# A causal convolution and a two-layer feed-forward block: accumulators copied out in the order they lie, and part of the activation moved from VectorE to ScalarE

## The chip, the cores and the metric

The kernel runs on one core of a Trainium2 chip. Its time is what the device takes for one execution, in microseconds (us); the kernel before has a median of 2262.58 us over three runs (2262.18 to 2262.81). A core has TensorE (PE; PEld is its weight load), VectorE (DVE), ScalarE (ACT), GpSimd (POOL) and SyncE (SP, which here issues nearly all transfers). Each engine works through its own list of instructions in order, and waits where an instruction needs another engine's result.

## The reference

Input x has 8 sequences of 4096 tokens with 192 channels in fp32. Each of 8 groups of 24 channels has a causal convolution of 7 taps whose weights are a softmax. A feed-forward layer follows on all 32768 tokens:

```python
h = x @ w_in                       # 192 -> 2048
beta = 1.0
neg = h <= -beta
pos = h >= beta
g = np.where(pos, h, np.where(neg, 0.0, (h + beta) ** 2 / (4.0 * beta)))
return (g @ w_out).astype(np.float32)   # 2048 -> 192
```

The function g equals max(h, (clip(h, -1, 1)/2 + 1/2)^2). It also equals max(h, min(relu(h/2 + 1/2)^2, 1)).

## The kernel before

The tokens are cut into 64 superblocks of 512, and the 2048 hidden channels into 8 pairs of tiles of 128. One step, numbered q, treats one pair for one superblock; there are 512 steps, and two superblocks (sixteen steps) make a block, because the convolution's work is planned over two superblocks. "Step k" below means q modulo 16.

In step q TensorE runs `mm1(q)` (L422), which puts h for two tiles (128 x 1024) in PSUM, and then `mm2(q - 2)` (L462), which adds the second layer's products to four accumulator banks, accm twice and accr twice. The fp32 values are split in a high and a low fp32r part, so mm1 has eighteen matmuls and mm2 twenty, on half the rows of the array each, two at a time. There are two buffers for h, three each for g, gh and gl.

The activation of a step is made by five instructions over 128 x 1024 values: `act_clip` on VectorE (L473, reads h from PSUM), `act_square` on ScalarE (L479, square of g/2 + 1/2), `act_max` on VectorE (L484, reads h again and gives its buffer back), `act_hi` on ScalarE (L491, the cast to the high part gh) and `act_lo` on VectorE (L497, the low part gl). The last two belong to q - 1. In the main loop the order on ScalarE is thus cast(q - 1), square(q), and on VectorE clip(q), low part(q - 1), max(q).

Around these the loop places the convolution for later tokens (`conv_slot`, by tables of step numbers: products on ScalarE at L219 and L226, sums on GpSimd at L230, transposes on VectorE at L147, the split into parts at L248 and L262, whose halves SP swaps with transfers).

When a superblock's eight steps are done, `evac` copies its four accumulator banks to SBUF (L513, ScalarE) behind the square of step 1 or 9, so that the mm2 of step 2 or 10 can start the next sums. From the third superblock on, TensorE works on the tokens in another order than they lie in memory (`turns`, `both`), and L513 restores an order: it reads a bank in sequence and writes each value to a place that is far from the one before. GpSimd adds the two halves (L515), `evac_rest` moves 64 channels (L525), and `store` turns 32 x 32 tiles around on VectorE (L538) and writes 32 channels at a time with one transfer (L542).

In the first eight steps the kernel makes the activation in another way, which has its own helpers: relu(h/2 + 1/2) and square on ScalarE (L757, L759), and `most` on VectorE (L764), which takes min(g, 1) and the max with h in one instruction.

Of the kernel before, what the change touches and what calls it, by code (L numbers as in the profile page):

```python
# [13 lines left out]
AF = mybir.ActivationFunctionType  # L14
# [6 lines left out]
SQ = 32  # L21
# [9 lines left out]
def lightconv_then_ffn(ctx: ExitStack, tc: tile.TileContext, x, weight, w_in, w_out, out):  # L31
# [24 lines left out]
    nc = tc.nc  # L56
# [8 lines left out]
    NPAIR = NF // 2  # L65
# [44 lines left out]
    def load_unit(c, u, engs=None):  # L110
        ta, tb = 2 * c * TB, (2 * c + 1) * TB
        if u == "rb":
            return load_raw([tb, tb, tb + TB // 2, tb + TB // 2], [P, P + SQ, P, P + SQ], engs,
                            TB // 2)
        if u == "r":
            return load_raw([ta, ta, tb, tb], [P, P + SQ, P, P + SQ], engs)
        return load_raw([ta if u == "a" else tb] * 4, [0, SQ, 2 * SQ, 3 * SQ], engs)
# [5 lines left out]
    def let_go():  # L123

        if pending:
            out, a, b = pending.pop(0)
            nc.vector.memset(warm, 0.0)
            nc.gpsimd.memset(warm, 0.0)
            nc.gpsimd.tensor_add(out, a, b)


    NF32 = 2 * NPAIR
# [257 lines left out]
    NQ = NSB * NPAIR  # L390
    hs, g32, gs, ghs, gls, accs = {}, {}, {}, {}, {}, {}
# [8 lines left out]
    def in_turns(s):  # L400
        return s * NPAIR >= NF32

    def mm1(q):

        s, j = divmod(q, NPAIR)

        if q == 0:
            h = hs[q] = [ps_o.tile([P, TB], F32, name=n) for n in ("accr1", "accm0")]
        else:
            h = hs[q] = ps_h.tile([P, 2, TB], F32, name="h")  # L410
            h = [h[:, e, :] for e in range(2)]

        if s == 0:
            mms = [(WI[j], us, [xop[s][u] for u in us]) for us in ("ns", "sn", "rr")]
        else:
            mms = [(W[j][:, part], u + u, [xop[s][u, x]] * 2) for u in "nsr"
                   for part, x in ((0, "hi"), (1, "hi"), (0, "lo"))]
        for n, (w, us, x) in enumerate(mms):
            for e in range(2):
                c0 = COL[us[e]][e]  # L420
                to, of = (both(h[e]), turns(x[e][e])) if in_turns(s) else (h[e], x[e][e])
                nc.tensor.matmul(to, w[HALVES[e], c0:c0 + P], of,  # L422
                                 start=(n == 0), stop=(n == len(mms) - 1))
# [5 lines left out]
    def mm2_first(q):  # L429


        s, j = divmod(q, NPAIR)
        g, w = g32.pop(q), WF[j + LAG]
        if j == 0:
            new_accs(s)
        for e in range(2):
            for b in range(TB // P):
                a, c0 = "mr"[b // 2], b % 2 * D
                for i, half in enumerate(HALVES):
                    nc.tensor.matmul(accs[s][a, i][:, c0:c0 + D], g[half, e, b * P:(b + 1) * P],  # L440
                                     w[half, e, :], start=(j == 0 and e == 0 and b % 2 == 0),
                                     stop=(j == NPAIR - 1 and e == 1 and b % 2 == 1))
# [24 lines left out]
    def tiles(q):  # L467
        return [slice(0, 1), slice(1, 2)] if q == NQ - 1 else [slice(0, 2)]

    def act_clip(q):  # L470
        g = gs[q] = act.tile([P, 2, TB], F32, name="g", bufs=3)
        for e in tiles(q):
            nc.vector.tensor_scalar(out=g[:, e, :], in0=hs[q][:, e, :], scalar1=-1.0, scalar2=1.0,  # L473
                                    op0=ALU.max, op1=ALU.min)

    def act_square(q):
        g = gs[q]
        for e in tiles(q):
            nc.scalar.activation(g[:, e, :], g[:, e, :], AF.Square, bias=0.5, scale=0.5)  # L479

    def act_max(q):
        h, g = hs.pop(q), gs[q]
        for e in tiles(q):
            nc.vector.tensor_tensor(out=g[:, e, :], in0=h[:, e, :], in1=g[:, e, :], op=ALU.max)  # L484
        if q < NF32:
            g32[q] = gs.pop(q)

    def act_hi(q):
        gh = ghs[q] = act.tile([P, 2, TB], F32R, name="gh", bufs=3)
        for e in tiles(q):  # L490
            nc.scalar.copy(gh[:, e, :], gs[q][:, e, :])  # L491
# [9 lines left out]
    def evac(s):  # L501

        acc = accs.pop(s)
        n = slice(0, 2 * D if s * NPAIR < NF32 else TB)
        for a in "mr":
            t = [ob.tile([P, TB], F32, name="t", bufs=4) for _ in range(2)]
            y = ob.tile([P, TB], F32, name="sum")
            for i in range(2):
                to, of = t[i][:, n], acc[a, i][:, n]
                if in_turns(s):  # L510
                    to = to.rearrange("p (b o a) -> p a b o", b=2, o=2)
                    of = of.rearrange("p (a b o) -> p a b o", b=2, o=2)
                nc.scalar.copy(to, of)  # L513
            if s > 0:
                nc.gpsimd.tensor_add(y[:, n], t[0][:, n], t[1][:, n])  # L515
            else:
                late.append((y[:, n], t[0][:, n], t[1][:, n]))
            sums[s, a] = y
# [9 lines left out]
    def store(s, a, *engs):  # L528
        engs = engs or (nc.sync,)
        y = sums.pop((s, a))  # L530
        if s * NPAIR < NF32:
            t0 = s * TB + (0 if a == "m" else 2 * P)
            engs[0].dma_start(out=out[t0:t0 + 2 * P].rearrange("(b p) d -> p b d", p=P),
                              in_=y[:, 0:2 * D].rearrange("p (b d) -> p b d", b=2))
            return
        n = P if a == "m" else DR
        osb = ob.tile([P, TB // SQ, SQ], F32, name="osb")
        nc.vector.transpose(out=osb[0:n].rearrange("p j b -> p (j b)"), in_=y[0:n])  # L538
        for i in range(n // SQ):
            c0 = i * SQ + (0 if a == "m" else P)  # L540
            dst = out[s * TB:(s + 1) * TB, c0:c0 + SQ]
            engs[i % len(engs)].dma_start(out=dst.rearrange("(j a) b -> a j b", a=SQ),  # L542
                                          in_=osb[i * SQ:(i + 1) * SQ])

    def diagonal(t, *bases):
        nc.gpsimd.memset(t, 0.0)
# [195 lines left out]
    def parts_hi(q):  # L742
        for n, rest in PARTS.get(q, ()):
            chunks[n].hi(rest)
# [17 lines left out]
    def most(h, g):  # L762

        nc.vector.scalar_tensor_tensor(out=g, in0=g, scalar=1.0, in1=h, op0=ALU.min, op1=ALU.max)  # L764
# [75 lines left out]
    for q in range(NQ + DELAY):  # L840
        s, j = divmod(q, NPAIR)
        c, i = divmod(q, 2 * NPAIR)
        done = q - DELAY
        if q < NQ and i == 0 and c > 0:
            conv_b = conv_n["b"]
        if q < NQ and i == (0 if c > 0 else 4):
            conv_n = {}
            if c + 1 < NB:
                conv_n = {u: Conv(c + 1, u, load_unit(c + 1, u)) for u in "arb"}


        if q == NPAIR:
            mm2_first(done)
        if q < NQ:
            mm1(q)
        if done >= 0 and q != NPAIR:
            (mm2 if done >= NF32 else mm2_first)(done)

        if q < 2:
            (step_0, step_1)[q]()  # L860
        elif q < NPAIR:
            first_step(q)
        else:
            if q - 1 in gs:
                act_hi(q - 1)
            if q == NPAIR + 1:
                evac(0)
            if q == 2 * NPAIR - 2:
                pending.extend(late)
            if q < NQ:  # L870
                let_go()
                act_clip(q)
                act_square(q)
            if done % NPAIR == NPAIR - 1 and done >= NPAIR:
                (evac if done < NQ - 1 else evac_last)(done // NPAIR)
            parts_hi(q + 1)
            if q - 1 in gs:
                act_lo(q - 1, nc.vector)
            parts_lo(q, (True,))
            if q < NQ:  # L880
                let_go()
                act_max(q)
                parts_lo(q, (False,))
                conv_slot(i, conv_b, conv_n.get("a"), conv_n.get("r"))

            m, r = (DELAY, DELAY + 1) if s > 1 else (NPAIR - 2, NPAIR - 1)
            if q < NQ and j == m:
                evac_rest(s - 1)
                store(s - 1, "m")
            elif q < NQ and j == r:  # L890
                store(s - 1, "r")
        if q < NQ and i == 2 * NPAIR - 1 and conv_n:
            conv_n["b"].transpose()
        if q == NQ - 4:
            plain = ob.tile([P, TB // SQ, SQ], F32, name="osb").rearrange("p j b -> p (j b)")[:, 0:P]
            diagonal(plain, 0)
# [26 lines left out]
```

## Time and profile before

| What | Value |
|---|---|
| median of three runs | 2262.58 us (2262.18 to 2262.81) |
| the profiled execution | 2263.56 us, of which the span of its instructions is 2261.8 us |
| granted TensorE clock | 1.00 |
| busy: PE, DVE, ACT, POOL | 97%, 92%, 79%, 51% of the span |
| L513, 512 columns | 244 copies, 1079 ns (accm) and 1113 ns (accr) each |
| clip L473, max L484, low part L497 | 503, 503, 495 instructions; 1200, 1217, 1467 ns |
| square L479, cast L491 | 503, 495 instructions; 1058, 1046 ns |
| stores of 64 KB | 366, landing 1.9 us after issue (median) |

A row of the groups gives line, engine, operation, the names written and read, and after the bar the busy us, the mean ns of one, and how long the engine had stood idle before it and for whom. A row of the timeline begins with the start and the length in us, with idle time in square brackets. A row of the stretches gives the busy time of each engine with the number of its instructions.

### The profile page before, as it was taken

The numbers are of one execution on the slowest core, as the hardware profiler recorded it, in microseconds if no ns is written. First come the engines' busy times: TensorE is split into PE (matmuls) and PEld (weight loads), VectorE is DVE, ScalarE is ACT, GpSimd is POOL, SyncE is SP. The second block draws the span as 40 slices with busy tenths as digits, with TensorE's granted clock in tenths as the row PEclk, the third lists the DMA queues.
The fourth block names the chain that finished last, engine by engine and source line by source line (L and its number), as shares of the span: only waits on it lengthen the run. The fifth ranks groups of instructions, "written<-read, shape, count | busy, mean of one in ns | idle before, by whom it ended". The sixth has DMA issues, their size and how long they took to land.

```text
span 2261.8 us, 48144 instructions
## 1 busy us (share of the span) xinstructions
PE 2189.4 (97%) x19646; PEld 1862.2 (82%) x19646; DVE 2077.1 (92%) x1883; ACT 1785.3 (79%) x2153; POOL 1148.6 (51%) x868
## 2 busy tenths in 40 slices
PE   9999999999999999999999999999999999999999
PEld 6988888888888888888888888888888888888887
DVE  8899999999999999999999999999999999999998
ACT  7787877778877788777887787877878778788775
POOL 1455644556545565444654455644556445565451
PEclk9999999999999999999999999999999999999999
DMA  6222122221222212222122222222221222212211
GB/s 158 49 51 51 38 53 44 47 53 38 51 48 46 53 34 51 49 49 51 41 44 48 49 50 48 42 48 44 51 53 39 51 49 45 54 34 51 49 32 27
DMA packets 442125, 110.84 MB, mean 49 GB/s; under 512 B 410288, under 2 KB 417840, under 8 KB 441904
## 3 DMA queue, kind: packets, MB, share of 16 engines
q1 hardware_dynamic: 441744, 107.66, 24.2%
q8 instruction: 155, 2.54, 0.5%
q14 instruction: 66, 0.54, 0.1%
q10 hardware_dynamic: 160, 0.10, 0.0%
HBM read 32.84 MB, written 25.17 MB: 26 GB/s over the span
## 4 chain that ended last, share of the span: by engine, by line
DVE 26%; ACT 23%; PE 20%; issue 14%; POOL 12%; SPq 3%; DMA 1%; POOLq 0%; DVEq 0%; ACTq 0%
POOL y L230 11%; PE h L422 9%; DVE g L484 8%; ACT t L513 8%; DVE g L473 8%; DVE gl L497 7%; ACT g L479 6%; ACT gh L491 5%; PE accm L462 5%; PE accr L462 4%; DVE osb L538 2%; SPq L95 2%; ACT p L219 2%; POOL lo L252 2%; DMA raw<-in_x_dram 1%
## 5 line engine op out<-in xcount | busy, mean ns | idle before, releaser
L230 POOL TENSOR_TENSOR y<-y,p 128x512 f32<-128x512 f32 x546 | 799.8, 1465 | 757.9 <-DVE g L484 539.8
L497 DVE TENSOR_TENSOR gl<-g,gh 128x1024 fp32r<-128x1024 f32 (+1 forms) x497 | 727.5, 1464 | 151.4 <-ACT gh L491 140.4
L491 ACT CAST gh<-g 128x1024 fp32r<-128x1024 f32 (+1 forms) x497 | 519.2, 1045 | 253.9 <-DVE g L484 248.7
L422 PE MATMUL h<-hi,w 64*128 64x512 f32 x4032 | 701.6, 377 | 0.0
L479 ACT ACTIVATE g<-g 128x1024 f32<-128x1024 f32 (+1 forms) x505 | 533.6, 1057 | 161.3 <-DVE g L473 151.0
L462 PE MATMUL accm<-gh,w 64*128 64x512 f32 x3968 | 614.0, 381 | 48.0 <-ACT t L513 48.0
L484 DVE TENSOR_TENSOR g<-h,g 128x1024 f32<-128x1024 f32 (+1 forms) x505 | 613.4, 1215 | 8.2 <-ACT g L479 4.4
L473 DVE TENSOR_SCALAR g<-h 128x1024 f32<-128x1024 f32 (+1 forms) x505 | 604.8, 1198 | 11.6 <-PE h L422 10.8
L422 PEld LDWEIGHTS h<-hi,w 64*128 64x128 f32 x4032 | 522.7, 186 | 50.5
L462 PEld LDWEIGHTS accm<-gh,w 64*128 64x128 f32 x3968 | 439.1, 186 | 128.4 <-ACT t L513 78.3
L422 PE MATMUL h<-lo,w 64*128 64x512 f32 x2016 | 541.7, 376 | 0.0
L462 PE MATMUL accr<-gh,wr 64*128 64x512 f32 x1984 | 390.4, 382 | 15.7 <-ACT t L513 15.7
L462 PE MATMUL accm<-gl,w 64*128 64x512 f32 x1984 | 380.0, 382 | 3.2
L219 ACT ACTIVATE p<-xT,wk 128x512 f32<-128x512 f32 x562 | 375.1, 710 | 0.0
L462 PE MATMUL accr<-gl,wr 64*128 64x512 f32 x1984 | 374.1, 376 | 0.0
L422 PEld LDWEIGHTS h<-lo,w 64*128 64x128 f32 x2016 | 330.4, 186 | 25.8
L462 PEld LDWEIGHTS accr<-gh,wr 64*128 64x128 f32 x1984 | 251.9, 186 | 63.0 <-ACT t L513 40.2
L422 PE MATMUL h<-rhi,w 64*128 64x512 f32 x992 | 293.6, 376 | 0.0
L422 PE MATMUL h<-rh,w 64*128 64x512 f32 x992 | 293.5, 376 | 0.0
L462 PEld LDWEIGHTS accm<-gl,w 64*128 64x128 f32 x1984 | 248.6, 186 | 44.3 <-DVE gl L497 23.1
L462 PEld LDWEIGHTS accr<-gl,wr 64*128 64x128 f32 x1984 | 256.8, 186 | 26.1 <-DVE gl L497 0.2
L515 POOL TENSOR_TENSOR sum<-t 128x512 f32<-128x512 f32 (+1 forms) x124 | 158.5, 1279 | 153.3 <-ACT t L513 153.3
(141 smaller groups left out, 2008.6 us busy)
## 6 DMA issues: line engine op xcount, KB each, us to landing
out_dram<-osb SPq DMA_DIRECT2D x366, 64.0 KB, 1.9
raw<-in_x_dram SPq DMA_DIRECT2D x334, 68.0 KB, 2.4
hi<-hi SPq DMA_DIRECT2D x126, 128.0 KB, 2.3
lo<-lo SPq DMA_DIRECT2D x126, 128.0 KB, 2.3
rhi<-rh SPq DMA_DIRECT2D x62, 128.0 KB, 2.2
rlo<-rl SPq DMA_DIRECT2D x62, 128.0 KB, 2.3
words<-in_moe_w_in_dram SPq DMA_DIRECT2D x16, 192.0 KB, 4.0
words<-in_moe_w_out_dram SPq DMA_DIRECT2D x8, 384.0 KB, 4.0
```

The costliest lines, as they stand in the source:

```text
L95: (engs[i] if engs else nc.sync).dma_start(out=raw[i * SQ:(i + 1) * SQ, lo:n // SQ + 1, :], in_=src.rearrange("(j a) b -> a j b", a=SQ),)
L219: nc.scalar.mul(p, self.xT[:, SH + k:SH + k + TB], wk[:, self.wsel, k:k + 1])
L230: nc.gpsimd.tensor_add(y, y, self.product(k))
L422: nc.tensor.matmul(to, w[HALVES[e], c0:c0 + P], of, start=(n == 0), stop=(n == len(mms) - 1))
L462: nc.tensor.matmul(both(accs[s][a, i]), st, turns(g[HALVES[i], e, :]), start=(j == 0 and n == first[a]), stop=(j == NPAIR - 1 and n == las ...
L473: nc.vector.tensor_scalar(out=g[:, e, :], in0=hs[q][:, e, :], scalar1=-1.0, scalar2=1.0, op0=ALU.max, op1=ALU.min)
L479: nc.scalar.activation(g[:, e, :], g[:, e, :], AF.Square, bias=0.5, scale=0.5)
L484: nc.vector.tensor_tensor(out=g[:, e, :], in0=h[:, e, :], in1=g[:, e, :], op=ALU.max)
L491: nc.scalar.copy(gh[:, e, :], gs[q][:, e, :])
L497: eng.tensor_sub(gl[:, e, :], g[:, e, :], gh[:, e, :])
L513: nc.scalar.copy(to, of)
L515: nc.gpsimd.tensor_add(y[:, n], t[0][:, n], t[1][:, n])
```

## The change

There are two edits, and the steps in which the first holds are the last four of a block, 12 to 15, from the third superblock on and without the last two q (122 steps).

In these steps g is made as in the first eight: ScalarE forms relu(h/2 + 1/2) from h, then squares it in place, and VectorE takes `most` in the place of clip and max. The relu stands in front of the cast of q - 1 in ScalarE's list.

The second edit takes the reordering out of the copies. The values keep TensorE's order through the sum and the turning of tiles, and the store's address pattern puts each token where it belongs; the runs it writes are 32 floats as before.

```diff
+    BY_ACT = (12, 13, 14, 15)
+    def by_act(q):
+        return q % (2 * NPAIR) in BY_ACT and NF32 <= q < NQ - 2
+
     def act_clip(q):
         g = gs[q] = act.tile([P, 2, TB], F32, name="g", bufs=3)
+        if by_act(q):
+            nc.scalar.activation(g, hs[q], AF.Relu, bias=0.5, scale=0.5)
+            return
...
     def act_square(q):
         g = gs[q]
+        if by_act(q):
+            nc.scalar.activation(g, g, AF.Square)
+            return
...
     def act_max(q):
         h, g = hs.pop(q), gs[q]
-        for e in tiles(q):
+        if by_act(q):
+            most(h, g)
+        for e in () if by_act(q) else tiles(q):
...
             for i in range(2):
-                to, of = t[i][:, n], acc[a, i][:, n]
-                if in_turns(s):
-                    to = to.rearrange("p (b o a) -> p a b o", b=2, o=2)
-                    of = of.rearrange("p (a b o) -> p a b o", b=2, o=2)
-                nc.scalar.copy(to, of)
+                nc.scalar.copy(t[i][:, n], acc[a, i][:, n])
...
-            engs[i % len(engs)].dma_start(out=dst.rearrange("(j a) b -> a j b", a=SQ),
-                                          in_=osb[i * SQ:(i + 1) * SQ])
+            engs[i % len(engs)].dma_start(
+                out=dst.rearrange("(e j k) b -> k e j b", e=4, k=SQ // 4),
+                in_=osb[i * SQ:(i + 1) * SQ])
...
         else:
+            ahead = q < NQ and by_act(q)
+            if ahead:
+                act_clip(q)
             if q - 1 in gs:
                 act_hi(q - 1)
...
                 let_go()
-                act_clip(q)
+                if not ahead:
+                    act_clip(q)
                 act_square(q)
```

ScalarE's list in steps 1 and 2 of a block, before: cast, square, the four copies out of the accumulators (their shape is that of the reordering), and the next cast and square.

```order
L491 CAST gh<-g 128x1024
L479 ACTIVATE g<-g 128x1024
L513 COPY t<-accm_4456 128x128x4
L513 COPY t<-accm_4457 128x128x4
L513 COPY t<-accr_4458 128x128x4
L513 COPY t<-accr_4459 128x128x4
L491 CAST gh<-g 128x1024
L479 ACTIVATE g<-g 128x1024
```

The same place of the change:

```order
L505 CAST gh<-g 128x1024
L491 ACTIVATE g<-g 128x1024
L523 COPY t<-accm_4456 128x512
L523 COPY t<-accm_4457 128x512
L523 COPY t<-accr_4458 128x512
L523 COPY t<-accr_4459 128x512
L505 CAST gh<-g 128x1024
L491 ACTIVATE g<-g 128x1024
```

Nothing has moved there; only the shape of the copies differs. (Line 491 is the cast before, and the square in the change.)

ScalarE's list at steps 11 to 13 of a block, before: products of the convolution, then cast and square of each step, with the cast of the convolution's result (L262) in step 13.

```order
L219 ACTIVATE p<-xT,wk 128x512 x2
L491 CAST gh<-g 128x1024
L479 ACTIVATE g<-g 128x1024
L491 CAST gh<-g 128x1024
L479 ACTIVATE g<-g 128x1024
L262 CAST rh<-y 128x512
```

The change at the same place:

```order
L219 ACTIVATE p<-xT,wk 128x512 x2
L479 ACTIVATE g<-h 128x1024
L505 CAST gh<-g 128x1024
L488 ACTIVATE g<-g 128x1024
L479 ACTIVATE g<-h 128x1024
L505 CAST gh<-g 128x1024
L488 ACTIVATE g<-g 128x1024
L262 CAST rh<-y 128x512
```

Line 479 of the change is the relu; it stands ahead of each step's cast. VectorE's list in the same steps of the change, where each step had three instructions and now has two:

```order
L548 STREAM_TRANSPOSE osb<-sum 64x512
L511 TENSOR_TENSOR gl<-g,gh 128x1024
L775 SCALAR_TENSOR_TENSOR g<-g,h 128x1024
L511 TENSOR_TENSOR gl<-g,gh 128x1024
L775 SCALAR_TENSOR_TENSOR g<-g,h 128x1024
L263 TENSOR_TENSOR rl<-y,rh 128x512
```

The clip is gone; `most` (L775) follows the low part directly.

## The prediction

> **What bounds the kernel now.** I read the page first, then stretches of one block of sixteen steps, then the engines' rows in the stretches where TensorE falters. A step is one q: eighteen matmuls of the first layer (mm1), twenty of the second for q - 2 (mm2).
>
> ```profile
> span 2261.8 us, 48144 instructions
> PE 2189.4 (97%) x19646; PEld 1862.2 (82%) x19646; DVE 2077.1 (92%) x1883; ACT 1785.3 (79%) x2153; POOL 1148.6 (51%) x868
> ```
>
> TensorE and VectorE both look like the bound, so averages don't decide it. The stretches below are, in order: a whole block (steps 0 to 15), steps 0-1, step 2, steps 3-5, step 6, step 9, step 10, steps 12-15.
>
> ```profile
> core 0: us, PE busy (x) PEld busy (x) DVE busy (x) ACT busy (x) POOL busy (x), PEclk, DMA share, GB/s
> 993.62:1063.57 69.95, 67.69 (x610) 57.44 (x608) 64.68 (x57) 55.76 (x67) 37.02 (x29) 1.00 0.24 47
> 993.62:1001.82 8.20, 8.20 (x78) 7.19 (x76) 8.06 (x9) 5.85 (x8) 1.29 (x1) 1.00 0.48 76
> 1001.82:1007.22 5.40, 4.74 (x40) 3.62 (x38) 3.42 (x3) 5.40 (x7) 2.00 (x2) 1.00 0.00 0
> 1007.22:1019.53 12.31, 12.31 (x116) 10.82 (x114) 12.21 (x11) 8.92 (x12) 8.07 (x7) 1.00 0.20 34
> 1019.53:1024.24 4.71, 4.58 (x41) 3.62 (x39) 4.08 (x5) 4.37 (x7) 1.59 (x2) 1.00 0.02 4
> 1032.44:1036.69 4.25, 4.25 (x40) 3.52 (x38) 4.25 (x4) 3.59 (x7) 3.44 (x4) 1.00 0.16 38
> 1036.69:1043.06 6.37, 4.90 (x39) 3.44 (x38) 4.31 (x4) 6.37 (x8) 5.24 (x4) 1.00 0.25 59
> 1047.16:1063.57 16.41, 16.41 (x154) 14.42 (x152) 16.32 (x15) 9.90 (x11) 4.68 (x7) 1.00 0.37 71
> 200.00:400.00 200.00, 193.95 (x1744) 165.12 (x1746) 184.39 (x161) 158.35 (x188) 101.46 (x77) 1.00 0.24 47
> 2000.00:2200.00 200.00, 193.24 (x1738) 163.87 (x1736) 184.41 (x160) 160.98 (x191) 104.44 (x74) 1.00 0.22 43
> ```
>
> Steps 12-15 take 16.41 us, 4.10 each, TensorE never waiting; steps 0-1 and 3-5 give the same 4.10. That is its pace, and sixteen such steps are 65.6 us. The block takes 69.95: 4.33 too long, of which step 2 has 1.30, step 6 has 0.61, step 9 has 0.15 and step 10 has 2.27. The last two rows, the first and last of ten like them after the first 200 us, show the same density early and late, so every block is like this one. In steps 12-15, where the new ScalarE work goes, nothing is lost today. The loss of step 2:
>
> ```profile
> 1001.69 1.07 ACT L479 ACTIVATE g<-g 128x1024 f32<-128x1024 f32 x1
> 1002.66 1.95 ACT L513 COPY t<-accm 128x512 f32<-128x512 f32 x2
> 1003.77 0.48 PE L462 MATMUL accm<-gh,w 64*128 64x512 f32 x1
> 1004.18 1.23 DVE L473 TENSOR_SCALAR g<-h 128x1024 f32<-128x1024 f32 x1 [0.17 <-PE h L422]
> 1004.42 2.01 ACT L513 COPY t<-accr 128x512 f32<-128x512 f32 x2
> 1004.66 1.13 PE L462 MATMUL accm<-gh,w 64*128 64x512 f32 x7 [0.41 <-ACT t L513]
> 1006.23 1.05 ACT L491 CAST gh<-g 128x1024 fp32r<-128x1024 f32 x1
> 1006.48 0.70 PE L462 MATMUL accr<-gh,wr 64*128 64x512 f32 x3 [0.26 <-ACT t L513]
> 1007.31 1.55 DVE L497 TENSOR_TENSOR gl<-g,gh 128x1024 fp32r<-128x1024 f32 x1 [1.91 <-ACT gh L491]
> ```
>
> The next sums want the four accumulator banks that ScalarE is still copying out (L513). TensorE stops for accm and again for accr, and VectorE idles 1.91 us because the cast L491 stands behind the copies. Step 10 is the same, later in the step:
>
> ```profile
> 1037.54 1.06 ACT L479 ACTIVATE g<-g 128x1024 f32<-128x1024 f32 x1
> 1038.51 1.95 ACT L513 COPY t<-accm 128x512 f32<-128x512 f32 x2
> 1039.60 0.48 PE L462 MATMUL accm<-gh,w 64*128 64x512 f32 x1 [0.80 <-ACT t L513]
> 1043.15 1.56 DVE L497 TENSOR_TENSOR gl<-g,gh 128x1024 fp32r<-128x1024 f32 x1 [2.01 <-ACT gh L491]
> ```
>
> **The copies.** The change lets L513 write t in the order in which it reads.
>
> ```profile
> L513 ACT COPY t<-accr 128x512 f32<-128x512 f32 x122 | 123.0, 1113 | 0.0
> L513 ACT COPY t<-accm 128x512 f32<-128x512 f32 x122 | 118.9, 1079 | 0.0
> L513 ACT COPY t<-accm 128x384 f32<-128x384 f32 x4 | 1.7, 469 | 0.0
> L165 ACT COPY xT<-h x1: 587/587/587, 5.5 to 5.5; 128x512 f32<-128x512 f32 x1
> ```
>
> The same line without the reordering (384 columns) takes 469 ns; a plain copy of 512 columns out of PSUM takes 587 (L165). The bounds for the new copy are 469 and 1113 ns (no change); I take 587, the same shape. Successive ScalarE instructions here start about 0.1 us before the one ahead ends (1001.69 + 1.07 against 1002.66), so a new copy occupies 0.49. 122 + 122 rows are 61 evacuations, 30 in step 2 and 31 in step 10.
>
> Step 2: copies start as now, 0.84 after the step's start at 1001.82, and end at 1.42, 1.91, 2.40 and 2.89. mm2 starts at 1.95 (half a step of 38 matmuls: 18 x 0.108) and finds the first bank free and the second all but; accr is wanted after twelve more, at 3.24, and is free. Left: 0.03 of 1.30, so 1.27 x 30 = 38 us.
>
> Step 10: copies start 1.81 after the step (1038.51 - 1036.70). Ends: 2.40, 2.89, 3.38, 3.87. mm2 wants the first bank at 1.94 and waits 0.5, then 0.3 for the second and about 0.1 more where a pair of matmuls runs one by one; with rounding 1.0. accr is wanted at about 4.2 and free. So 1.27 x 31 = 39 us. It doesn't go to nothing, because square (L479) in front of the copies ends late there for other reasons: the step inherits VectorE's lag.
>
> **Step 6** is a chain, not the copies:
>
> ```profile
> 1019.10 0.73 DVE L147 STREAM_TRANSPOSE xT<-raw 128x544 f32<-128x544 f32 x1
> 1019.87 0.72 ACT L226 ACTIVATE y<-xT,wk 128x512 f32<-128x512 f32 x1 [1.34 <-DVE xT L147]
> 1020.50 1.04 ACT L491 CAST gh<-g 128x1024 fp32r<-128x1024 f32 x1
> 1021.57 1.23 DVE L497 TENSOR_TENSOR gl<-g,gh 128x1024 fp32r<-128x1024 f32 x1 [0.63 <-ACT gh L491]
> ```
>
> VectorE ran 12.21 of the 12.31 us of steps 3-5, so it starts this chain as early as it left the wait of 1.91 behind. With the cast 1.5 us earlier (four copies by 0.49 instead of 3.57 us) it is 1.5 to 1.7 earlier, while TensorE asks 1.27 earlier: 0.3 of the 0.61 goes, 10 us over 31 blocks. Step 9 is a chain of the same sort: I give it 1 us.
>
> **ScalarE in steps 12-15.** 122 steps (31 blocks of four, less the last two q).
>
> ```profile
> L473 DVE TENSOR_SCALAR g<-h 128x1024 f32<-128x1024 f32 x503 | 603.5, 1200 | 11.2 <-PE h L422 10.3
> L757 ACT ACTIVATE g<-h 128x1024 f32<-128x1024 f32 x7 | 7.1, 1017 | 2.4 <-PE h L422 2.4
> L484 DVE TENSOR_TENSOR g<-h,g 128x1024 f32<-128x1024 f32 x503 | 612.1, 1217 | 8.2 <-ACT g L479 4.4
> L764 DVE SCALAR_TENSOR_TENSOR g<-g,h 128x1024 f32<-128x1024 f32 x7 | 8.5, 1216 | 0.0
> 1055.11 1.04 ACT L491 CAST gh<-g 128x1024 fp32r<-128x1024 f32 x1 [1.35 <-DVE g L484]
> ```
>
> VectorE loses 122 clips of 1.20 us (146), ScalarE gains 122 relus of 1.02 (124), about what the copies give it back (244 x 0.51 = 124). The max costs 1216 ns in its new form and 1217 in the old; the square stays. On the path this is worth 0: TensorE is at its pace there, and ScalarE waits 1.35 us for VectorE's max. It is not free by itself, since relu(q) stands in front of the cast of q - 1. Walked from a step's start: h is ready at 2.35 (1004.18 in step 2, when the clip that had waited for it began, against 1001.82), relu to 3.4, cast to 4.4, square to 5.4, low part 4.4 to 5.65, max to 6.75. The next step's mm2 starts at 4.10 + 1.95, and wants that low part after eight matmuls more, at 6.9, 1.25 us later; h is wanted back at 8.2 (two steps), 1.4 after the max. So TensorE doesn't wait; nor does step 2 come earlier, since VectorE catches up with TensorE in these steps today as well. If the cover were gone, each us of lateness would cost 4 x 31 = 124 us.
>
> **The stores** keep count, size and order on SP, and write the same runs of 32 floats; only the outer dimension goes from 32 to 8.
>
> ```profile
> out_dram<-osb SPq DMA_DIRECT2D x366, 64.0 KB, 1.9
> ```
>
> Bounds: 1.9 us as now, and six in a line each twice as long, 23 us. An osb buffer is rewritten after eight steps, 33 us: 0 either way. The Trainium skill (DMA: Bandwidth & Descriptors, section on why a DMA increments its semaphore by 16) speaks against this edit: the number of DMA engines that share a transfer divides the outermost dimension, so 8 would carry what 16 do now. By that rule the landing would rise towards twice 1.9 us; by the row it would stay, and the sum is the same.
>
> Sum: 38 + 39 + 10 + 1 = 88. The profiled execution took 2263.56 us; 2263.56 - 88 = 2175. It lies 1 us above the median of the runs, 2262.58, which the forecast may ignore.
>
> **Rivals.** *All stalls go.* The copies of step 10 start earlier because VectorE lags less, and step 6 clears: 1.30 x 30 + 3.03 x 31 = 133, so 2131 us. For it: VectorE loses 4.8 us of work a block. Against: none of that in steps 2-11, where the lag arises.
>
> *VectorE becomes the bound of steps 2-11.* It is busy 64.68 - 8.06 - 16.32 = 40.3 us there, TensorE needs 41.0. With waits that stay (0.63 and 0.17 in the rows above, about 0.5 after either set of copies, where 1.91 and 2.01 stand now) it needs 42.1, and my forecast for those steps is 41.0 + 1.5 = 42.5: hardly any room. The low parts L497 swing between 1.2 us and the 1.55 above. If the closer packing makes four of them per block 0.4 longer, TensorE pays up to 1.5 us in 31 blocks: 47 back, 2222 us. The Trainium skill (SBUF — State Buffer, "Who interferes with whom") has a reason for the swing: a VectorE instruction with two SBUF inputs and a GpSimd instruction that reads SBUF lock each other out. By that rule shifted GpSimd adds decide it, and 2222 is the bad side.
>
> *The copies stay at 1.1 us*, since bank traffic and not the order of writing makes them slow: then all terms vanish, 2263. Against: 469 ns on the same line and bank.
>
> *Slower: relu holds up the cast.* In steps 12-15 relu waits for mm1 in ScalarE's queue, and the cast behind it is what VectorE's low part and then mm2 wait for. It decides from 1.25 us of lateness on. One relu more than that (1.02 us) costs 122 x 1.02 = 124, against the 88 won: 2299 us. For it: the queue is in order. Against: the walk above has relu in it already, with the cast at 3.4 where the max of q - 1 would have let it start at 2.7, and mm2 still has its 1.25 us.
>
> **How the numbers follow.** Forecast 2175, chance 0.52, own range 2150 to 2200. All stalls go 0.15; VectorE bound 0.20; copies unchanged 0.06; relu in front 0.07. The range 2135 to 2225 takes in most of the first two rivals and leaves out the last two and half of the first. A change under 0.2%, 4.5 us, can't be told from none. Faster: the first three, 0.87; same 0.06; slower 0.07.
>
> **What would show it.** The copy row at 0.59 us, not 1.1; step 2 at 4.1 us and step 10 at about 5.1, not 6.4; the idle time of L497 after the copies at about 0.5 instead of 1.91 and 2.01; steps 12-15 still at 16.4 us together, with VectorE busy about 12 of them. If steps 12-15 are longer, relu in front was wrong; if steps 3-9 are, VectorE. Stores that land late with no wait on them are harmless; a wait on osb would not be.

## The result, and the profile after

The changed kernel takes 2170.27 us (median of four runs, 2170.16 to 2170.41) against 2262.69 us before; the ratio is 0.9591, with a 95% interval of 0.9575 to 0.9608. The forecast was 2175. The profiled execution took 2170.17 us, 93.4 less than that of before.

The head of the page of the changed kernel, its span and the busy time of each engine:

```profile
span 2168.2 us, 47869 instructions
PE 2152.2 (99%) x19646; PEld 1891.3 (87%) x19646; DVE 1954.5 (90%) x1761; ACT 1784.8 (82%) x2275; POOL 1138.4 (53%) x868
```

VectorE lost 123 us of work, and not the 146 of 122 clips, in the main because its low parts grew from 1467 to 1501 ns. ScalarE neither won nor lost any: what the copies gave back went to the relus. The same block as before (its sixteen steps begin at 954.65 now), in stretches for the whole, steps 0-1, step 2, steps 3-5, step 6, step 9, step 10 and steps 12-15:

```profile
954.65:1021.50 66.85, 66.52 (x610) 57.51 (x608) 60.62 (x52) 55.73 (x71) 36.73 (x29) 1.00 0.25 48
954.65:962.85 8.20, 8.20 (x79) 7.19 (x77) 7.91 (x8) 5.80 (x8) 1.28 (x1) 1.00 0.42 66
962.85:966.95 4.10, 4.10 (x41) 3.60 (x38) 3.68 (x4) 4.10 (x7) 2.27 (x2) 1.00 0.00 0
966.95:979.25 12.30, 12.30 (x116) 10.79 (x114) 12.29 (x12) 8.58 (x12) 8.03 (x7) 1.00 0.21 34
979.25:983.59 4.34, 4.34 (x41) 3.71 (x39) 3.71 (x4) 4.34 (x7) 1.21 (x2) 1.00 0.01 3
991.79:996.03 4.24, 4.24 (x40) 3.52 (x38) 4.24 (x4) 3.59 (x7) 3.43 (x4) 1.00 0.15 36
996.03:1001.00 4.97, 4.64 (x41) 3.52 (x39) 4.46 (x5) 4.97 (x8) 4.89 (x4) 1.00 0.33 75
1005.10:1021.50 16.40, 16.40 (x154) 14.41 (x152) 12.20 (x11) 13.26 (x16) 4.41 (x7) 1.00 0.39 73
```

A block went from 69.95 to 66.85 us. Step 2 is at TensorE's pace (5.40 to 4.10), step 10 went from 6.37 to 4.97, step 6 from 4.71 to 4.34, step 9 stayed at 4.24 (4.25 before). Steps 12-15 take 16.40 us as before, although VectorE has 12.2 us of work there now and had 16.3.

The groups that answer to those of before: copies (L523), relu (L479 now) and the low part (L511), with busy us, mean ns, and idle time ahead:

```profile
L523 ACT COPY t<-accr 128x512 f32<-128x512 f32 x122 | 66.2, 604 | 0.0
L523 ACT COPY t<-accm 128x512 f32<-128x512 f32 x122 | 64.3, 578 | 0.0
L479 ACT ACTIVATE g<-h 128x1024 f32<-128x1024 f32 x122 | 124.4, 1019 | 76.0 <-PE h L422 76.0
L511 DVE TENSOR_TENSOR gl<-g,gh 128x1024 fp32r<-128x1024 f32 x495 | 743.0, 1501 | 181.1 <-ACT gh L505 168.2
```

Step 10 on the timeline (start, length):

```profile
996.88 1.06 ACT L491 ACTIVATE g<-g 128x1024 f32<-128x1024 f32 x1
997.84 1.05 ACT L523 COPY t<-accm 128x512 f32<-128x512 f32 x2
998.46 1.61 PE L462 MATMUL accm<-gh,w 64*128 64x512 f32 x8 [0.32 <-ACT t L523]
998.78 1.08 ACT L523 COPY t<-accr 128x512 f32<-128x512 f32 x2
1000.85 2.07 DVE L511 TENSOR_TENSOR gl<-g,gh 128x1024 fp32r<-128x1024 f32 x1 [0.38 <-ACT gh L505]
```

The copies start 1.81 us after the step (997.84 - 996.03), the same place as before, and the pair takes 1.05 where it took 1.95. TensorE waits for the accm banks alone; accr is free in time. The low part waits 0.38 us and not 2.01.

### The profile page after: what moved, and what is told of

Its sections match the earlier page's. It is cut to its first block, busy times and chain, and to the rows that moved or that the text cites. A ratio compares the mean times of both kernels' runs of the same rounds, so it can differ in the third digit from the quotient of the medians.

```text
span 2168.2 us, 47869 instructions
## 1 busy us (share of the span) xinstructions
PE 2152.2 (99%) x19646; PEld 1891.3 (87%) x19646; DVE 1954.5 (90%) x1761; ACT 1784.8 (82%) x2275; POOL 1138.4 (53%) x868
## 4 chain that ended last, share of the span: by engine, by line
PE 38%; ACT 19%; DVE 18%; POOL 13%; issue 11%; DMA 0%; POOLq 0%; SPq 0%; DVEq 0%; ACTq 0%
PE h L422 17%; PE accm L462 11%; POOL y L230 11%; PE accr L462 7%; DVE g L482 6%; ACT g L491 6%; DVE g L498 5%; ACT gh L505 4%; ACT t L523 3%; DVE gl L511 3%; ACT p L219 3%; DVE g L775 2%; DVE osb L548 2%; POOL lo L252 2%; ACT g L479 1%
## 5 line engine op out<-in xcount | busy, mean ns | idle before, releaser
L511 DVE TENSOR_TENSOR gl<-g,gh 128x1024 fp32r<-128x1024 f32 (+1 forms) x497 | 744.2, 1498 | 181.2 <-ACT gh L505 168.2
L462 PE MATMUL accm<-gh,w 64*128 64x512 f32 x3968 | 601.5, 378 | 9.7 <-ACT t L523 9.5
L422 PE MATMUL h<-lo,w 64*128 64x512 f32 x2016 | 535.4, 376 | 0.0
L462 PEld LDWEIGHTS accm<-gh,w 64*128 64x128 f32 x3968 | 450.1, 186 | 74.1 <-ACT t L523 30.0
L491 ACT ACTIVATE g<-g 128x1024 f32<-128x1024 f32 x383 | 405.1, 1058 | 120.2 <-DVE g L482 115.1
L482 DVE TENSOR_SCALAR g<-h 128x1024 f32<-128x1024 f32 x383 | 457.6, 1195 | 15.0 <-PE h L422 14.9
L498 DVE TENSOR_TENSOR g<-h,g 128x1024 f32<-128x1024 f32 x383 | 463.9, 1211 | 4.6 <-ACT g L491 4.2
L462 PE MATMUL accr<-gh,wr 64*128 64x512 f32 x1984 | 370.5, 376 | 0.0
L422 PEld LDWEIGHTS h<-rhi,w 64*128 64x128 f32 x992 | 184.5, 186 | 14.1
```

The source lines that it names most:

```text
L422: nc.tensor.matmul(to, w[HALVES[e], c0:c0 + P], of, start=(n == 0), stop=(n == len(mms) - 1))
L462: nc.tensor.matmul(both(accs[s][a, i]), st, turns(g[HALVES[i], e, :]), start=(j == 0 and n == first[a]), stop=(j == NPAIR - 1 and n == las ...
L511: eng.tensor_sub(gl[:, e, :], g[:, e, :], gh[:, e, :])
```

## The experiments

Each ratio is to the kernel before on the same chip, whose median lay between 2262.69 and 2263.62 us. Differences between two changed kernels are taken from their medians, so one of 1 us says nothing.

**Each half of the change by itself.** First the copies and stores without any relu on ScalarE:

```diff
-    BY_ACT = (12, 13, 14, 15)
+    BY_ACT = ()
```

> The copies and stores of the change, and no step with relu on ScalarE. Theory A (the copies carry the whole gain, since in steps 12 to 15 TensorE was at its pace before): 2168 to 2173 us, a block of 66.8 us, steps 12 to 15 at 16.4 us together. Rival B (VectorE's relief of four clips is needed once the copies are short, because VectorE's 64.7 us of work nearly fill a block of 65.6): 2190 us or more, with steps 12 to 15 or 2 to 11 longer by 0.7 us a block.

2170.26 us, ratio 0.9592 (0.9576 to 0.9608): the changed kernel's time to a hundredth of a us. Its block and its steps 12-15:

```profile
954.55:1021.39 66.84, 66.51 (x611) 57.55 (x608) 64.85 (x57) 52.49 (x67) 36.58 (x29) 1.00 0.26 49
1004.99:1021.39 16.40, 16.40 (x155) 14.41 (x152) 16.29 (x15) 9.92 (x12) 4.39 (x7) 1.00 0.39 71
```

VectorE works 64.85 of 66.84 us and is still not what sets the end. So the copies carry the gain, and rival B falls. Then the other half, relu in steps 12-15 with the copies of before (and the stores' pattern of before, not shown again):

```diff
-                nc.scalar.copy(t[i][:, n], acc[a, i][:, n])
+                to, of = t[i][:, n], acc[a, i][:, n]
+                if in_turns(s):
+                    to = to.rearrange("p (b o a) -> p a b o", b=2, o=2)
+                    of = of.rearrange("p (a b o) -> p a b o", b=2, o=2)
+                nc.scalar.copy(to, of)
```

> Relu on ScalarE in steps 12 to 15, with the copies and the stores of before. Theory A: no change, 2260 to 2265 us, step 2 and step 10 still 5.4 and 6.4 us long, while VectorE is busy for about 12.2 of the 16.4 us of steps 12 to 15. Rival B (VectorE's lag is what makes the copies start late): step 10 gets shorter by 0.5 us or more, 2245 us or less.

2259.94 us, ratio 0.9987 (0.9978 to 0.9997): 3 us, small, but the executions (2259.51 to 2261.05) don't overlap with those of before (2262.39 to 2263.82). Step 2 and step 10:

```profile
999.84:1005.13 5.29, 4.64 (x42) 3.52 (x39) 3.28 (x3) 5.29 (x7) 2.01 (x2) 1.00 0.00 0
1034.56:1040.94 6.38, 4.90 (x41) 3.43 (x40) 4.30 (x4) 6.38 (x8) 5.24 (x4) 1.00 0.25 58
```

Step 10 hasn't moved, so rival B falls here too. Step 2 is 0.11 us shorter, and 30 times that is the 3 us: with the old copies a little of VectorE's lag did reach step 2, where the prediction had nothing. In the changed kernel this is gone, because step 2 has nothing left to lose.

**The place of relu.** Behind the cast and not in front of it:

```diff
-            ahead = q < NQ and by_act(q)
+            ahead = False
```

> The whole change, but relu stands behind the cast of q - 1 in ScalarE's list, not in front of it. Theory A (both orders leave over 1 us in hand in steps 12 to 15): 2168 to 2173 us. Rival (the place in front matters): relu behind comes 1.3 us later, so the max gives h back later, and steps 12 to 15 exceed 16.4 us: 2180 us or more.

2231.51 us, ratio 0.9860 (0.9845 to 0.9875): 61 us of the gain are lost. My theory expected nothing here, and was wrong; the rival was right. TensorE's weight loads for the next h now wait 88 times for the max to give its buffer back, which they never do in the change, and the block grows from 66.85 to 68.89 us (the rows are the wait, the block and step 2):

```profile
PEld h L422 <- DVE g L775: 30.7, 88, 0.4
```
```profile
979.82:1048.71 68.89, 68.17 (x610) 57.94 (x608) 60.70 (x52) 56.11 (x71) 36.64 (x29) 1.00 0.25 47
988.46:993.52 5.06, 4.66 (x41) 3.72 (x41) 4.56 (x5) 5.04 (x8) 3.13 (x3) 1.00 0.01 3
```

ScalarE's and VectorE's rows at step 15, in order of time:

```profile
1044.34 1.05 ACT L505 CAST gh<-g 128x1024 fp32r<-128x1024 f32 x1 [0.78 <-DVE g L775]
1045.30 1.02 ACT L479 ACTIVATE g<-h 128x1024 f32<-128x1024 f32 x1
1046.35 1.06 ACT L488 ACTIVATE g<-g 128x1024 f32<-128x1024 f32 x1
1048.69 1.05 ACT L505 CAST gh<-g 128x1024 fp32r<-128x1024 f32 x1 [1.29 <-DVE g L775]
```
```profile
1043.09 1.22 DVE L775 SCALAR_TENSOR_TENSOR g<-g,h 128x1024 f32<-128x1024 f32 x1 [0.79 <-ACT g L488]
1047.44 1.22 DVE L775 SCALAR_TENSOR_TENSOR g<-g,h 128x1024 f32<-128x1024 f32 x1 [0.78 <-ACT g L488]
```

Cast of q - 1, relu of q, square of q, max of q, and then the cast of q, which needs that max: a closed ring of four instructions on two engines. It turns once in 4.35 us (1048.69 - 1044.34), and TensorE's step is 4.10. Each turn is 0.25 us too long, and steps 13 to 1 lose 0.97 us of the block's 2.04 in this way. The lag is handed on into step 2, which is 5.06 us long and pays another 0.96. With relu in front of the cast, it waits for h alone and not for the max of q - 1. The ring is then cast, square and max, which by the starts in the rows above would turn in about 3.3 us (an estimate: 0.96 + 1.09 + 1.25).

**One more us between relu and cast,** to measure what the order of the change has in hand:

```diff
             if ahead:
                 act_clip(q)
+            if ahead:
+                for _ in range(1):
+                    nc.scalar.copy(gs[q], gs[q])
             if q - 1 in gs:
                 act_hi(q - 1)
```

> The whole change, with one more ScalarE copy of g onto itself (128 x 1024, about 1.0 us) between relu and cast in steps 12 to 15. Theory A (the low part has 1.25 us in hand there): 2168 to 2175 us, steps 12 to 15 at 16.4 us together. Rival (nothing in hand): each of the 122 steps pays 1.0 us, 2290 us.

2212.89 us, ratio 0.9774 (0.9758 to 0.9791): 43 us, neither nothing nor 124. Steps 2 and 13:

```profile
980.49:985.32 4.83, 4.63 (x40) 3.51 (x38) 4.27 (x5) 4.74 (x8) 2.83 (x3) 1.00 0.01 3
1027.71:1032.25 4.54, 4.54 (x41) 3.81 (x39) 2.64 (x3) 4.51 (x5) 1.39 (x4) 1.00 0.18 29
```

Step 13 pays 0.44, since in step 12 relu stands behind two products:

```profile
1025.29 1.33 ACT L219 ACTIVATE p<-xT,wk 128x512 f32<-128x512 f32 x2
1026.52 1.00 ACT L479 ACTIVATE g<-h 128x1024 f32<-128x1024 f32 x1
```

The relu starts 2.9 us after its step (which began at 1023.61, 4.10 before the 1027.71 of step 13), not at the 2.35 of the walk. Step 2 pays 0.73: the max that VectorE makes for step 15 comes a us later, and the transpose, the clip, the square and the copies behind it pass all of it on (the copies start 1.67 us after step 2 began, and 0.70 in the change). Steps 6 and 15 pay about 0.1 each, which makes up the rest of the 43 us. So 1.25 us roughly holds for a step in the middle of the four, not for the first, and not for what follows the last.

**What is left of step 6.** Step 4 joins the steps with relu on ScalarE:

```diff
-    BY_ACT = (12, 13, 14, 15)
+    BY_ACT = (4, 12, 13, 14, 15)
```

> The whole change, with step 4 added to the steps with relu on ScalarE. Theory A (what is left of step 6, 0.21 us, is VectorE's lag at the transpose of step 4, and ScalarE idles enough there): the transpose comes 0.5 us earlier, step 6 falls to 4.10 us, 31 x 0.21 = 7 us less: 2163 to 2165 us. Rival (ScalarE has no room in step 4, the cast of step 3 comes later): step 6 stays or another step grows, 2170 us or more.

2156.20 us, ratio 0.9527 (0.9513 to 0.9542): 14 us faster than the change, twice what was expected. Steps 6, 9 and 10:

```profile
974.16:978.26 4.10, 4.10 (x41) 3.60 (x39) 3.48 (x4) 4.10 (x7) 1.45 (x2) 1.00 0.07 16
986.46:990.56 4.10, 4.10 (x41) 3.60 (x38) 4.10 (x4) 3.60 (x6) 3.29 (x4) 1.00 0.19 45
990.56:995.40 4.84, 4.83 (x40) 3.69 (x38) 4.33 (x5) 4.84 (x8) 4.76 (x4) 1.00 0.30 70
```

Step 6 lost its 0.24, step 9 its 0.14, and step 10 0.13 of its 0.87: one relu in step 4 shortens all three, so VectorE's lag is one and the same from step 4 to step 10. In step 4 the relu fills a gap of ScalarE. Its row on the timeline of the changed kernel, where it idles 1.06 us ahead of the cast:

```profile
974.53 1.05 ACT L505 CAST gh<-g 128x1024 fp32r<-128x1024 f32 x1 [1.06 <-DVE g L498]
```

The same place on the timeline with relu in step 4, where the cast follows at once:

```profile
968.31 1.02 ACT L479 ACTIVATE g<-h 128x1024 f32<-128x1024 f32 x1
969.37 1.05 ACT L505 CAST gh<-g 128x1024 fp32r<-128x1024 f32 x1
```

**What is left of step 10.** The accm copies go ahead of the square in step 9 (`early` marks it), the accr copies stay behind it:

```diff
+                if early:
+                    evac(done // NPAIR, "m")
                 act_square(q)
-            if done % NPAIR == NPAIR - 1 and done >= NPAIR:
+            if early:
+                evac(done // NPAIR, "r")
+            elif done % NPAIR == NPAIR - 1 and done >= NPAIR:
```

> The whole change, and in step 9 the two accm copies stand ahead of the square, the two accr copies behind it. Theory A (what is left of step 10, 0.87 us, is the place of the copies behind the square): the accm copies start 0.95 us earlier, at 0.85 after the step's start, and the second bank is free at 1.9, when mm2 wants it; accr is wanted at 3.2 and copied by 3.9, so 0.6 of the wait moves to accr unless the square's 1.0 is made up: step 10 at 4.2 to 4.8 us, 2150 to 2168 us. Rival (the copies wait for the sums themselves, or VectorE's max behind the later square holds h back): step 10 at 4.97 us or more, 2170 us or more.

2161.84 us, ratio 0.9550 (0.9535 to 0.9564), 8 us faster than the change. In the profile step 10 lost 0.38 us and step 6 0.2, while step 13 grew by 0.27, which no theory had. Both edits together:

> Relu on ScalarE in step 4 too, and the accm copies ahead of the square in step 9. Theory A (the two rests have two causes): step 6 and step 9 at 4.10 us as with step 4 alone (2156 us), and step 10 shorter by what the copies' place gives, 0.1 to 0.6 us x 31: 2138 to 2153 us. Rival (one lag behind both): no better than the better of the two alone, 2156 us.

2147.42 us, ratio 0.9487 (0.9473 to 0.9502), 23 us faster than the change, as much as the two alone give in sum (14 + 8). Step 10 with the accm copies alone moved, and steps 10 and 13 with both:

```profile
992.67:997.26 4.59, 4.59 (x39) 3.72 (x38) 3.76 (x4) 4.25 (x7) 4.51 (x4) 1.00 0.35 81
```
```profile
986.78:991.05 4.27, 4.27 (x41) 3.51 (x38) 3.45 (x4) 3.94 (x7) 4.19 (x4) 1.00 0.30 71
999.25:1003.60 4.35, 4.35 (x42) 3.70 (x39) 2.91 (x2) 3.36 (x5) 2.02 (x5) 1.00 0.21 32
```

So the rest of step 10 had two causes, the lag and the place of the copies. Step 13 is 0.25 too long with both. I put that down to the relu of step 12, and took the relus of steps 12 to 15 out (against the kernel with both):

```diff
-    BY_ACT = (4, 12, 13, 14, 15)
+    BY_ACT = (4,)
```

> Relu on ScalarE in step 4 alone, none in steps 12 to 15, and the accm copies ahead of the square in step 9. Theory A (in step 12 relu stands behind the products and holds up the cast of step 11, which costs step 13 0.27 us in the run with both; elsewhere in 12 to 15 it brings nothing): step 13 at 4.10 us, 31 x 0.27 = 8 us less than with both: 2137 to 2142 us. Rival (relief in steps 13 to 15 is needed once the other steps are at their pace): 2147 us or more.

2146.48 us, ratio 0.9483 (0.9467 to 0.9498), the lowest of all. Theory A missed, since 8 us were expected, and the rival's bound of 2147 us was missed by half a us. The kernel with both ran in 2146.83 to 2149.37 us and this one in 2146.01 to 2146.85, so they can hardly be told apart. The block with both, then the block and steps 10 and 13 without the relus in 12 to 15:

```profile
945.77:1011.80 66.03, 66.03 (x610) 57.58 (x608) 59.01 (x51) 56.81 (x73) 37.44 (x29) 1.00 0.26 49
```
```profile
945.22:1011.26 66.04, 66.04 (x610) 57.68 (x608) 62.33 (x56) 53.52 (x67) 39.80 (x29) 1.00 0.26 50
986.23:990.76 4.53, 4.53 (x41) 3.69 (x39) 3.72 (x4) 4.20 (x7) 4.45 (x4) 1.00 0.35 80
998.96:1003.06 4.10, 4.10 (x41) 3.60 (x38) 4.10 (x4) 2.08 (x3) 3.54 (x5) 1.00 0.22 34
```

Step 13 is at the pace, as expected, and step 10 has grown by the same 0.26: the loss has moved. The traces show a way, which no run tested. With both edits TensorE waits in step 13, and from there to step 10 of the next block the two matmuls of a pair start together; without that wait they start 0.2 us apart, and h is complete 0.2 us later. VectorE's clip of step 2, which waits for h, with both and then without the relus:

```profile
956.12 1.23 DVE L482 TENSOR_SCALAR g<-h 128x1024 f32<-128x1024 f32 x1 [0.26 <-PE h L422]
```
```profile
955.77 1.23 DVE L482 TENSOR_SCALAR g<-h 128x1024 f32<-128x1024 f32 x1 [0.47 <-PE h L422]
```

Step 2 began 8.20 us after the block, so the clip comes 2.15 us after it with both and 2.35 without. The copies of step 10 then start 0.48 and 0.75 us after their step (medians of 28 blocks). In step 3 a low part and a sum of GpSimd also meet in another order (it stands at the end of this document), but in the one block of the 28 where they meet as with both, step 10 still takes 4.46 us, so the order has little part in it.

**All sixteen steps on ScalarE** (`BY_ACT = tuple(range(16))`), a single execution, so without an interval:

> The whole change with relu on ScalarE in all sixteen steps. Theory A (ScalarE is then full: 55.7 us of a block plus 12 relus that occupy 0.95 each are 67.1 us, over the present block of 66.85, and its list has no room to wait): a block of 68 us or more, 2205 to 2300 us. Rival (VectorE is what matters, it falls to 47 us a block): 2165 us or less.

2286.82 us, beside 2263.12 before, as theory A has it. VectorE falls to 45.3 us in a block of 70.70, ScalarE rises to 65.5, and the block is 3.85 us longer than that of the change. ScalarE is not quite full; what the list lacks is room to wait, and VectorE's low parts wait 785 us for its casts in all, where they wait 168 in the change:

```profile
1005.39:1076.09 70.70, 67.88 (x610) 58.33 (x608) 45.29 (x40) 65.53 (x84) 33.56 (x29) 1.00 0.25 46
```

**The stores with the address pattern of before,** so that the stores' own share shows (the tokens of a superblock then land in the wrong places):

```diff
-                out=dst.rearrange("(e j k) b -> k e j b", e=4, k=SQ // 4),
+                out=dst.rearrange("(j a) b -> a j b", a=SQ),
```

> The whole change, but the stores keep the address pattern of before (32 outermost, not 8), so the tokens of a superblock land in another order. Theory A (the stores are off the path, whatever they take): 2168 to 2173 us, while the transfers count 2928 packets more and the stores of a superblock are through in about half the time. Rival (stores on half the engines hold something up): 2165 us or less.

2170.36 us, ratio 0.9587 (0.9573 to 0.9601): no difference. The queue's packets, first of this kernel and then of the change:

```profile
q1 hardware_dynamic: 441744, 107.66, 25.3%
```
```profile
q1 hardware_dynamic: 438816, 107.65, 25.9%
```

The change has 2928 packets fewer, 8 for each of 366 stores. The profile of the change gives no landing times, but its packets do: from the issue of the first of four stores in a row to the end of their last data packet it takes 4.3 us, and 3.0 us with the pattern of before (medians of 58 and 59 such fours). So the stores do take longer, by less than the expected factor of two, and no engine pays for it. One wait on osb was a sign to look for: GpSimd's, 5.4 us once near the end in the change. With the old pattern GpSimd waits 3.9 us there for VectorE instead, and the time is the same.

## Why the prediction was right

| Term | Predicted | Measured |
|---|---|---|
| a copy of 512 columns | 587 ns | 578 and 604 ns |
| step 2 | 1.27 x 30 = 38 us | 1.30 x 30 = 39 us |
| step 10 | 1.27 x 31 = 39 us | 1.40 x 31 = 43 us |
| step 6 | 10 us | 0.37 x 31 = 11 us |
| step 9 | 1 us | 0 |
| relu in steps 12-15 | 0 | 0 (the copies alone: 2170.26 us) |
| stores | 0 | 0 (the pattern of before: 2170.36 us) |
| sum | 88 us | 93.4 us |

*The copies.* The price from L165 held. Most of the missing 4 us of step 10 is a rounding: 0.5 + 0.3 + 0.1 is 0.9 us of waiting, and the prediction took 1.0; TensorE loses 0.87 there. The last 0.03 is the distance from one copy's start to the next, since two copies take 1.05 us and not 1.08. The copies' place, 1.81 us after the step, was the same before and after. The prediction read it off the old trace and gave no reason why the lag behind it should keep its size, so that part was in some measure luck.

*Step 6* was the chain that the prediction named; relu in step 4 removed it. Here I stopped too early: what I treated as separate rests in steps 6, 9 and 10 is in part one lag, and one relu at its head is worth 14 us, where the same relu four times at its tail is worth none.

*ScalarE in steps 12-15* was worth 0 as forecast, and for the reason given: TensorE was at its pace there, and without the relus the next block begins no later.

*The rivals.* "All stalls go" failed on step 10 as argued. "VectorE becomes the bound" came near: steps 2 to 11 took 42.25 us (66.85 - 8.20 - 16.40), and the rival had counted 42.1 for VectorE. The lag that relu in step 4 removed cost 14 us, and it was there before; the 47 us on top did not come, although the low parts got longer (2.07 in step 10, where 1.56 stood). The prediction had misread how far they swing, going by rows of 1.2 to 1.56 us. In the kernel before, 90 of the 495 already took more than 1.6 us, this one for instance:

```profile
1011.66 2.31 DVE L497 TENSOR_TENSOR gl<-g,gh 128x1024 fp32r<-128x1024 f32 x1
```

"The copies stay at 1.1 us" is refuted by the rows of L523. "Relu holds up the cast" cost nothing, but the reasoning on it had the danger the wrong way round. The prediction asked what relu in front delays, and gave it 1.25 us in hand; that roughly holds in the middle of the four steps only, as the added us showed. It didn't ask what relu behind would do, and that is where 61 us lie.

## What to carry to other kernels

Look for the steps in which the bounding engine really waits, and price an edit by what reaches them. VectorE's 123 us less of work were worth nothing behind the waits, in steps 12 to 15, and one step's share of it was worth 14 us ahead of them, in step 4. When an operation changes engine, write down the ring of instructions in which each needs the one ahead (here cast, relu, square, max) and compare one turn with the step; its place in the in-order list decides whether it is in the ring. A reordering costs where it is done: ScalarE paid nearly half of each copy (1079 and 1113 ns against 578 and 604) for an order that the store's address pattern makes at no cost in time. Whether the distance between the writes or the shape of the pattern made the copies slow was not separated.

## What the runs showed of the hardware that was not expected

A VectorE low part and a GpSimd sum that meet are not slowed in equal shares. In the two places below the one that starts first runs at its normal length, and the other pays. The same place, step 3, in the kernel with both edits, VectorE's row and GpSimd's:

```profile
962.01 2.21 DVE L511 TENSOR_TENSOR gl<-g,gh 128x1024 fp32r<-128x1024 f32 x1
```
```profile
961.87 1.27 POOL L536 TENSOR_TENSOR sum<-sum,t 64x512 f32<-64x512 f32 x1
```

and in the kernel with relu in step 4 alone:

```profile
961.49 1.20 DVE L511 TENSOR_TENSOR gl<-g,gh 128x1024 fp32r<-128x1024 f32 x1
```
```profile
961.51 2.32 POOL L536 TENSOR_TENSOR sum<-sum,t 64x512 f32<-64x512 f32 x1
```

A start 0.14 us behind GpSimd costs VectorE 1.0 us, and a start 0.02 us ahead costs GpSimd as much. In the trace of the change, 274 of the 495 low parts start while a GpSimd instruction runs: each takes what is left of that instruction and 1.08 us more. The other 221 take 1.19 to 1.23 us. The Trainium skill (SBUF — State Buffer, "Who interferes with whom") states such an exclusive lock, and these numbers agree. The recorded start does not always tell who wins: in the kernel with relu in step 4 alone, 30 low parts that start 0.44 to 0.47 us behind a sum of the convolution run in 1.20 us, and the sum takes 2.8. Why is open.

Of the packets of 4 bytes each store has 16 in the kernel before and 8 in the change, which is all of the difference of 2928. That agrees with a rule of the Trainium skill that the prediction weighed (DMA: Bandwidth & Descriptors, on why a DMA increments its semaphore by 16): one completion packet per engine used, so 8 engines where 16 were.
